# Second products ahead of the third pass, an earlier weight split and three relus on VectorE in a fused attention and mixture-of-experts kernel

## The chip, the cores and the metric

The kernel runs on one core of one Trainium2 chip. The core has TensorE (PE, matrix products into PSUM), VectorE (DVE), ScalarE (ACT), GpSimd (POOL) and SyncE (SP, which here only issues transfers). Each works through its own instructions in its own order, and semaphores tie them together. The metric is the device time of one execution in microseconds; the time of a kernel is the median over its runs.

## The reference

Polynomial attention without a softmax, and then a dense mixture of four experts on its output. Shapes: 4 batches, 4 heads, 1088 positions of 32 values, so 4352 tokens of 128 values; w1 is 4 x 128 x 1024 and w2 is 4 x 1024 x 128, all float32.

```python
phi(x) = outer(S1 @ x, S2 @ x).reshape(64)
kv = einsum('bhsf,bhsd->bhfd', phi(k), v);  z = sum(phi(k), axis=2)
x  = (phi(q) @ kv) / (phi(q) @ z + 1e-6)      # then heads side by side: (4352, 128)
p  = domain_probs / (domain_probs.sum(-1) + 1e-9)
out = sum over e of p[:, e] * (relu(x @ w1[e]) @ w2[e])
```

## The kernel before, in words

The 4352 tokens are worked in 11 chunks (128, 448, 512, seven times 448, 128). A chunk goes through 16 steps, four for each expert e; step i makes two 128-wide blocks of hidden values, j = 0 and j = 1. So (20,1) below is the second block of step 20, and steps 16 to 31 are chunk 1: 16 to 19 expert 0, 20 to 23 expert 1, 24 to 27 expert 2. `NQ` is 16, `NP` is 4.

**First product.** In chunks 1 to 9 the product x @ w1 is made of three fast passes on pieces of the operands (xa, xb, xd and wa, wb, wd). Function `first` issues the first two passes for (i,j) on TensorE (L1133, L1134), then ScalarE scales the PSUM tile in place (L1135). The third pass (L1182, in `third`) adds onto the scaled tile. It is issued one half step later, so that other matmuls lie between: within `first` for (i,j), `third()` issues the third pass of the half step before, and after it ScalarE takes the relu (L1190 into `hid`, or L1185 into `ha`; VectorE then makes the low parts `hb`, L1159, and `hd`, L1162, in `lower`).

**Second product.** The hidden blocks are multiplied by w2 later, from a list `due` sorted by half step. `to_due` enters them; `behind(at)` issues what is due by half step `at`. It is called through `between(0)` after the first half of a step and again after `first`. Chunk 0 is worked in plain float32 (L1111 relu, L245 products, L1218 on VectorE, L1223 the store of the result tile `end`); its last products are due in steps 16 and 17. In chunk 1 experts 0 and 1 have one float32 product per block (`whole`, L1231), due at half steps 2i + 3 + j. From expert 2 of chunk 1 on, each pair of blocks is dealt as short passes `a`, `b`, `d` and `x` by the table `DEAL` (L1250).

**Weights.** w2 is split into parts by `second_weight_parts(e)`, in two calls a few steps apart: the first makes the upper and lower parts (ScalarE L907, then two VectorE L910 `vab`, `vb`), the second the rest (L907, two L910 `vd`). `W2_AT` holds the steps of the two calls for the experts 2, 3, 0 and 1, and they are issued after `first` of that step:

```python
    W2_AT = (18, 19), (20, 21), (22, 23), (26, 32)
...
        for step in at:
            at_step(step, next_of(parts_of))
```

**Attention beside it.** The attention of later tokens is a list of pieces, `plan`, of which `work()` runs some in every half step. For one group of queries: a projection on TensorE (L245, `qT,sx`), a copy on ScalarE (L771, `qs`), a store to DRAM (`qd`, L773), loads in widened form (`qp`, L778, and `qb`, L783; ten issues on SyncE for the first group), two products on VectorE (L792, one for each half of the heads), the product with the key sums on TensorE (L245, `kvx,qp`), and division and transposes on VectorE. PSUM holds six banks for the tiles named `h` and one each for `o0` and `o1`. Order on each engine's queue is the order in which the program records the instructions; nothing is reordered later.

Of the kernel before, what the change touches and what calls it, by code (L numbers as in the profile page):

```python
# [12 lines left out]
ALU = mybir.AluOpType  # L13
ACTF = mybir.ActivationFunctionType
# [10 lines left out]
def kernel(  # L25
# [24 lines left out]
    nc = tc.nc  # L50
# [11 lines left out]
    NQ = E * FB // 2  # L62
# [20 lines left out]
        ("b", 1, 1, 16), ("d", 1, 1, 17), ("b", 2, 0, 16), ("d", 2, 0, 17), ("b", 2, 1, 17), ("d", 2, 1, 18),  # L83
        ("a", 3, 1, 17), ("b", 3, 0, 19), ("d", 3, 0, 19), ("b", 3, 1, 20), ("d", 3, 1, 20),
    ]
    W2_AT = (18, 19), (20, 21), (22, 23), (26, 32)
    TOKENS_AT = 11, 12

    CHUNKS = [P, 448, 512] + [448] * 7 + [P]
# [13 lines left out]
    def psum(pool, tag):  # L103
        return pool.tile([P, 512], F32, tag=tag, name=tag)
# [64 lines left out]
    def in_three(b):  # L169
        return b in THREE  # L170
# [76 lines left out]
    def both(out, weights, moving, **flags):  # L247

        for _ in range(2):
            on_side(lambda s: out[half[s], :], lambda s: weights[:, half[s]], lambda s: moving, **flags)  # L250
# [129 lines left out]
    def placed(c, n):  # L380

        for a, z, t, off in PLACES:
            lo, hi = max(c, a), min(c + n, z)
            if lo < hi:
                yield t[:, off + lo - a : off + hi - a], lo - c, hi - lo
# [526 lines left out]
    def weight_part(what, e, h):  # L912

        c = slice(F // 2 * h, F // 2 * (h + 1))
        w, a, b, d = (x[:, c] for x in (w1_of[e], wa[:, e], wb[:, e], wd[:, e]))
        if what == "a":
            split(a, w, 4096.0)
        elif what == "b":
            join(b, w, -4096.0, a.bitcast(F32), ALU.add)
        else:  # L920
            join(d, a.bitcast(F32), -R12, b.bitcast(F32), ALU.subtract)
# [134 lines left out]
    hid, acc, total = {}, {}, {}  # L1056
    NP = FB // 2

    def plain(m):
        return m in (0, NC - 1)  # L1060

    def whole(m, e):
        return m == 1 and e < E // 2

    def three_first(m, e):
        return not plain(m)
# [3 lines left out]
    def half_columns(i, hp, c):  # L1070

        e, f = divmod(i, NP)
        for j in range(2):
            both(
                hp[:, P * j + c : P * j + c + HP],
                w1_of[e][:, P * (2 * f + j) : P * (2 * f + j + 1)],
                x_first[:, c : c + HP],
                start=True,
                stop=True,
            )  # L1080

    def first(i, work, between=None):

        m, kq = steps[i]
        n, (e, f) = CHUNKS[m], divmod(kq, NP)
        if plain(m):
            third()
            lower()
            hd = hidden()
            hid[i] = [hd[:, n * j : n * j + n] for j in range(2)]  # L1090
            if i in begun_hp:
                hp = begun_hp.pop(i)
                half_columns(i, hp, HP)
            elif i in made_hp:
                hp = made_hp.pop(i)
            else:
                hp = psum(ps_h, "h")
                for j in range(2):
                    both(
                        hp[:, n * j : n * j + n],  # L1100
                        w1_of[e][:, P * (2 * f + j) : P * (2 * f + j + 1)],
                        (x_last if m else x_first)[:, :],
                        start=True,
                        stop=True,
                    )
            if m and kq % 2:
                nc.vector.tensor_scalar(
                    out=hd[:, 0 : 2 * n], in0=hp[:, 0 : 2 * n], scalar1=0.0, scalar2=None, op0=ALU.max
                )
            else:  # L1110
                nc.scalar.activation(hd[:, 0 : 2 * n], hp[:, 0 : 2 * n], ACTF.Relu)  # L1111
            work()
            work()
            return
        hid[i] = []
        if not three_first(m, e):
            ((x, _, _),) = placed(START[m], n)
            for j in range(2):
                hp = psum(ps_h, "h")[:, 0:n]
                nc.tensor.matmul(hp, w1_of[e][:, P * (2 * f + j) : P * (2 * f + j + 1)], x, start=True, stop=True)  # L1120
                u = hidden()[:, 0:n]
                nc.scalar.activation(u, hp, ACTF.Relu)
                hid[i].append(u)
                work()
                if j == 0:
                    between(0)
            return
        xa, xb, xd_ = (x[:, 0:n] for x in xparts[m])
        for j in range(2):
            k = 2 * f + j  # L1130
            g = psum(ps_h, "h")[:, 0:n]
            w = slice(P * k, P * (k + 1))
            nc.tensor.matmul(g, wa[:, e, w], xa, start=True, stop=False)  # L1133
            nc.tensor.matmul(g, wb[:, e, w], xb, start=False, stop=True)  # L1134
            nc.scalar.activation(g, g, ACTF.Copy, scale=1.0 + R12)  # L1135
            third()
            hid[i].append(None)
            begun.append((i, j, k, g, wd[:, e, w], xd_))

            if any(d[0] <= 2 * i + j and d[5] and d[5] + str(2 * (steps[d[3]][1] % NP) + d[4]) == last_of[1] for d in due):  # L1140
                between(j)
                lower()
                work()
            else:
                lower()
                work()
                if j == 0:
                    between(0)

    def hidden():  # L1150
        return mpool.tile([P, CW], F32, tag="hid", bufs=4, name="hid")
# [3 lines left out]
    def lower():  # L1155

        while to_lower:
            g, high, hb, both_of = to_lower.pop(0)
            nc.vector.scalar_tensor_tensor(out=hb, in0=g, scalar=0.0, in1=high, op0=ALU.max, op1=ALU.subtract)  # L1159
            if both_of:  # L1160
                a2, b2, d2 = both_of
                nc.vector.scalar_tensor_tensor(  # L1162
                    out=d2, in0=a2.bitcast(F32), scalar=R12, in1=b2.bitcast(F32), op0=ALU.mult, op1=ALU.subtract
                )
# [3 lines left out]
    def three_tiles(k, n):  # L1168

        t = split_at(k)  # L1170
        if t % 2 == 0:
            pair_of[0] = [
                mpool.tile([P, 2, CW], F32R, tag=f"h{i}", bufs=2, name=f"h{i}")[:, :, 0:n] for i in "abd"
            ]
        return tuple(x[:, t % 2] for x in pair_of[0]), pair_of[0] if t % 2 else None

    def third():

        while begun:
            i, j, k, g, w, x = begun.pop(0)  # L1180
            n = g.shape[-1]
            nc.tensor.matmul(g, w, x, start=False, stop=True, skip_group_check=True)  # L1182
            if in_three(k) and not whole(steps[i][0], steps[i][1] // NP):
                (ha, hb, hc), both_of = three_tiles(k, n)
                nc.scalar.activation(ha, g, ACTF.Relu, scale=NEAR)  # L1185
                to_lower.append((g, ha.bitcast(F32), hb, both_of))
                hid[i][j] = ha, hb, hc
            else:
                hid[i][j] = hidden()[:, 0:n]
                nc.scalar.activation(hid[i][j], g, ACTF.Relu)  # L1190

    def second(i, j=None):

# [152 lines left out]
    def at_step(step, *calls):  # L1346
        to_part.setdefault(step, []).extend(calls)
# [4 lines left out]
    for what, e, h, step in SPLITS:  # L1352
        at_step(step, lambda p=(what, e, h): weight_part(*p))
    for e, at in zip((2, 3, 0, 1), W2_AT):
        parts_of = second_weight_parts(e)
# [21 lines left out]
    due, closed = [], [None]  # L1377
# [16 lines left out]
    def to_due(i):  # L1394

        m, kq = steps[i]
        e, f = divmod(kq, NP)
        if plain(m):
            due.append((2 * i + 5, 2 * i, 0, i, None, None))
        elif whole(m, e):  # L1400
            due.extend((2 * i + 3 + j, 2 * i, j, i, j, None) for j in range(2))
        elif f == 0:
            for at, (p, slot) in enumerate(DEAL.items()):
                k = int(p[1])
                due.append((2 * i + slot, 2 * i, at, i + k // 2, k % 2, p[0]))
        due.sort(key=lambda d: d[:3])

    for i in range(len(steps) + LA):
        if i < len(steps):
# [11 lines left out]
            def work():  # L1421

                now[0] += 1
                if not NQ <= i < NQ + 2:
                    credit[0] = min(credit[0] + rate * rooms[min(now[0], len(rooms) - 1)], 0.5)
                if holds[0]:
                    credit[0] = max(credit[0], 0.01)
                while credit[0] > 0:
                    cost = piece()
                    credit[0] -= cost  # L1430
                    if not cost:
                        break

            first(i, work, lambda j: behind(2 * i + j))
            to_due(i)
            if kq == NQ - 4 and 0 < m < NC - 2:
                until_there(START[m + 1] + CHUNKS[m + 1])
# [57 lines left out]
```

## Time and profile before

| What | Value |
|---|---|
| Median of 3 runs | 451.99 us (451.21 to 453.21) |
| The profiled execution | 452.88 us, its span 450.0 us |
| Granted TensorE clock | 1.00 over the span |
| TensorE, VectorE, ScalarE, GpSimd busy | 99%, 80%, 74%, 27% |
| DMA, mean over the span | 85 GB/s |
| L1133, L1134, L1182, one pass of 448 columns | 468, 368, 371 ns busy, 0.20 us from start to start |
| L1231, one float32 product of 448 columns | two rows of 545 ns |
| L1135 and L1190 on ScalarE, 128x448 | 540 and 552 ns |
| L1159 on VectorE, 128x448 | 624 ns |
| L1279 on VectorE, copy of 128x448 out of PSUM | 610 ns |

The rows of a timeline read: start, busy time in us, engine, line, operation, written tile <- read tiles, shape, count; in brackets the idle time of the engine before it and who ended it. Rows of TensorE overlap, since matmuls are pipelined: the step from one start to the next tells more than the busy time. Where two steps in one row are merged (x2, x32), the time is that of all. SPq is SyncE's queue of transfers: its rows are the issues, not the transfers.

### The profile page before, as it was taken

The numbers are of one execution on the slowest core, as the hardware profiler recorded it, in microseconds if no ns is written. First come the engines' busy times: TensorE is split into PE (matmuls) and PEld (weight loads), VectorE is DVE, ScalarE is ACT, GpSimd is POOL, SyncE is SP. The second block draws the span as 40 slices with busy tenths as digits, with TensorE's granted clock in tenths as the row PEclk, the third lists the DMA queues.
The fourth block names the chain that finished last, engine by engine and source line by source line (L and its number), as shares of the span: only waits on it lengthen the run. The fifth ranks groups of instructions, "written<-read, shape, count | busy, mean of one in ns | idle before, by whom it ended". The sixth has DMA issues, their size and how long they took to land.

```text
span 450.0 us, 8678 instructions
## 1 busy us (share of the span) xinstructions
PE 444.5 (99%) x3021; PEld 369.3 (82%) x3021; DVE 358.6 (80%) x608; ACT 332.5 (74%) x702; POOL 121.5 (27%) x209
## 2 busy tenths in 40 slices
PE   8999999999999999999999999999999999999997
PEld 5887678777778888888888888888888888888886
DVE  5997689787988896888879869787779787787753
ACT  4477788677867886778688767787788788877741
POOL 7344133310323132212321312134123212321320
PEclk9999999999999999999999999999999999999999
DMA  7954741115223302252242142410320121018401
GB/s 197 296 145 142 189 118 58 30 30 129 93 58 88 120 23 79 51 129 70 66 124 27 22 113 78 119 49 21 95 52 28 33 45 41 22 34 217 158 2 28
DMA packets 53780, 38.45 MB, mean 85 GB/s; under 512 B 26921, under 2 KB 49897, under 8 KB 53737
## 3 DMA queue, kind: packets, MB, share of 16 engines
q1 hardware_dynamic: 53064, 37.77, 31.6%
q8 instruction: 23, 0.38, 0.4%
q0 software_dynamic: 448, 0.07, 0.2%
q14 instruction: 21, 0.16, 0.1%
q10 hardware_dynamic: 224, 0.07, 0.1%
HBM read 32.68 MB, written 5.21 MB: 84 GB/s over the span
## 4 chain that ended last, share of the span: by engine, by line
PE 94%; DVE 3%; DMA 1%; issue 1%; ACT 0%; SPq 0%; DVEq 0%
PE o L1250 39%; PE h L1182 13%; PE h L1133 13%; PE h L1134 13%; PE h L245 9%; PE o L245 3%; PE o L1231 3%; PE h L440 1%; DMA kn<-in_k_dram 1%; DVE hb L1159 1%; DVE qp L593 0%; DVE hd L1162 0%; DVE qa L882 0%; DVE rd L625 0%; DVE kp L456 0%
## 5 line engine op out<-in xcount | busy, mean ns | idle before, releaser
L1135 ACT ACTIVATE h<-h 128x448 f32<-128x448 f32 (+1 forms) x288 | 155.3, 540 | 79.0 <-PE h L1134 73.9
L1159 DVE SCALAR_TENSOR_TENSOR hb<-h,ha 128x448 fp32r<-128x448 f32 (+1 forms) x204 | 125.9, 624 | 55.8 <-ACT ha L1185 54.7
L1133 PE MATMUL h<-xa,wa 128*128 128x448 f32 (+1 forms) x288 | 134.9, 468 | 0.0
L1162 DVE SCALAR_TENSOR_TENSOR hd<-ha,hb 128x896 fp32r<-128x896 f32 (+1 forms) x102 | 116.0, 1137 | 8.2
L1185 ACT ACTIVATE ha<-h 128x448 fp32r<-128x448 f32 (+1 forms) x204 | 111.5, 547 | 0.0
L1182 PE MATMUL h<-xd,wd 128*128 128x448 f32 (+1 forms) x288 | 106.9, 371 | 0.2 <-ACT h L1135 0.2
L1134 PE MATMUL h<-xb,wb 128*128 128x448 f32 (+1 forms) x288 | 105.9, 368 | 0.0
L1289 POOL TENSOR_TENSOR ev<-ev,gate 128x256 f32<-128x256 f32 (+1 forms) x54 | 40.8, 756 | 219.8 <-DVE ev L1282 201.3
L1250 PE MATMUL o<-ha,vab 128*128 128x448 f32 (+1 forms) x204 | 76.4, 374 | 0.0
L1133 PEld LDWEIGHTS h<-xa,wa 128*128 128x128 f32 x288 | 54.2, 188 | 19.8 <-issue 14.6
L1134 PEld LDWEIGHTS h<-xb,wb 128*128 128x128 f32 x288 | 54.2, 188 | 19.5 <-issue 15.5
L1250 PE MATMUL o<-hid,w_sb 128*128 128x448 f32 (+1 forms) x136 | 63.0, 545 | 0.0
L1182 PEld LDWEIGHTS h<-xd,wd 128*128 128x128 f32 x288 | 54.0, 187 | 9.9 <-ACT h L1135 3.0
L1250 PE MATMUL o<-hd,vd 128*128 128x448 f32 (+1 forms) x204 | 58.8, 369 | 0.0
L1250 PE MATMUL o<-hb,vb 128*128 128x448 f32 (+1 forms) x136 | 49.9, 368 | 0.3 <-DVE hb L1159 0.3
L1291 POOL TENSOR_TENSOR total<-total,ev 128x256 f32<-128x256 f32 (+1 forms) x54 | 46.6, 864 | 4.2
L1190 ACT ACTIVATE hid<-h 128x448 f32<-128x448 f32 (+1 forms) x84 | 46.4, 552 | 0.2
L1250 PEld LDWEIGHTS o<-ha,vab 128*128 128x128 f32 x204 | 38.3, 188 | 4.2 <-issue 0.2
L1250 PEld LDWEIGHTS o<-hd,vd 128*128 128x128 f32 x204 | 38.1, 188 | 3.4
L1289 POOL TENSOR_TENSOR total<-ev,gate 128x256 f32<-128x256 f32 (+1 forms) x18 | 12.2, 699 | 75.6 <-issue 56.4
L1250 PEld LDWEIGHTS o<-hb,vb 128*128 128x128 f32 x136 | 25.5, 188 | 2.7 <-DVE hb L1159 0.7
L1250 PEld LDWEIGHTS o<-hid,w_sb 128*128 128x128 f32 x136 | 25.5, 188 | 2.5 <-DVE ev L1282 0.3
(141 smaller groups left out, 436.7 us busy)
## 6 DMA issues: line engine op xcount, KB each, us to landing
gate<-gates SPq DMA_DIRECT2D x24, 224.0 KB
kn<-in_k_dram SPq DMA_DIRECT2D x4, 544.0 KB
vn<-in_v_dram SPq DMA_DIRECT2D x16, 128.0 KB
w_last<-in_moe_w_dram SPq DMA_DIRECT2D x4, 512.0 KB
w_sb<-in_moe_w_dram SPq DMA_DIRECT2D x3, 512.0 KB
w_sb<-in_moe_w_dram SPq DMA_DIRECT2D x6, 256.0 KB
qp<-qd SPq DMA_DIRECT2D x6, 224.0 KB
qb<-qd SPq DMA_DIRECT2D x6, 224.0 KB
```

The costliest lines, as they stand in the source:

```text
L245: nc.tensor.matmul(out(s), weights(s), moving(s), **flags)
L1133: nc.tensor.matmul(g, wa[:, e, w], xa, start=True, stop=False)
L1134: nc.tensor.matmul(g, wb[:, e, w], xb, start=False, stop=True)
L1135: nc.scalar.activation(g, g, ACTF.Copy, scale=1.0 + R12)
L1159: nc.vector.scalar_tensor_tensor(out=hb, in0=g, scalar=0.0, in1=high, op0=ALU.max, op1=ALU.subtract)
L1162: nc.vector.scalar_tensor_tensor(out=d2, in0=a2.bitcast(F32), scalar=R12, in1=b2.bitcast(F32), op0=ALU.mult, op1=ALU.subtract)
L1182: nc.tensor.matmul(g, w, x, start=False, stop=True, skip_group_check=True)
L1185: nc.scalar.activation(ha, g, ACTF.Relu, scale=NEAR)
L1190: nc.scalar.activation(hid[i][j], g, ACTF.Relu)
L1250: nc.tensor.matmul(acc[m, e][o][:, 0:n], w, h, start=first_one, stop=last)
L1289: nc.gpsimd.tensor_tensor(out=to[:, x], in0=ev[:, x], in1=g[:, x], op=ALU.mult)
L1291: nc.gpsimd.tensor_tensor(out=total[m][:, x], in0=total[m][:, x], in1=ev[:, x], op=ALU.add)
```

## The change

1. In steps 16 and 17 `first` calls `between(j)` ahead of `third()`, so second products that are due come ahead of the third pass.
2. The first call of `second_weight_parts` for expert 1 moves from step 26 to step 24; the second stays in step 32.
3. In steps 20, 21 and 22 the relu of block j = 1 is a VectorE instruction.
4. The product of the last block of expert 1 (step 23, j = 1) is due one half step later, at 51 instead of 50.

```diff
-    W2_AT = (18, 19), (20, 21), (22, 23), (26, 32)
+    W2_AT = (18, 19), (20, 21), (22, 23), (24, 32)
...
             nc.scalar.activation(g, g, ACTF.Copy, scale=1.0 + R12)
+            if i < NQ + 2:
+                between(j)
             third()
...
                 hid[i][j] = hidden()[:, 0:n]
-                nc.scalar.activation(hid[i][j], g, ACTF.Relu)
+                if NQ + NP <= i < NQ + 2 * NP - 1 and j:
+                    nc.vector.tensor_scalar(
+                        out=hid[i][j], in0=g, scalar1=0.0, scalar2=None, op0=ALU.max
+                    )
+                else:
+                    nc.scalar.activation(hid[i][j], g, ACTF.Relu)
...
         elif whole(m, e):
-            due.extend((2 * i + 3 + j, 2 * i, j, i, j, None) for j in range(2))
+            late = e and f == NP - 1
+            due.extend((2 * i + 3 + j + (j if late else 0), 2 * i, j, i, j, None) for j in range(2))
```

The lines after these edits have higher numbers in the changed kernel; the text before the result uses those of the kernel before. The number of instructions and transfers of the whole program is the same; three change their engine.

## Prediction

> **What bounds the kernel now.** First the page's parts 1 and 2.
>
> ```profile
> PE 444.5 (99%) x3021; PEld 369.3 (82%) x3021; DVE 358.6 (80%) x608; ACT 332.5 (74%) x702; POOL 121.5 (27%) x209
> PEclk9999999999999999999999999999999999999999
> ```
>
> TensorE is busy 99% at full clock, so only its gaps can be won. Next, TensorE's timeline from 28 to 76 us. A 128x448 pass starts 0.20 us after the one before; larger steps between two starts are gaps.
>
> ```profile
> 29.38 0.37 PE L1134 MATMUL h<-xb,wb 128*128 128x448 f32 x1
> 29.95 0.47 PE L1182 MATMUL h<-xd,wd 128*128 128x448 f32 x1 [0.21 <-ACT h L1135]
> ...
> 31.86 0.36 PE L1134 MATMUL h<-xb,wb 128*128 128x448 f32 x1
> 32.23 0.47 PE L1182 MATMUL h<-xd,wd 128*128 128x448 f32 x1
> ...
> 60.59 0.36 PE L1134 MATMUL h<-xb,wb 128*128 128x448 f32 x1
> 60.96 0.47 PE L1182 MATMUL h<-xd,wd 128*128 128x448 f32 x1
> ...
> 67.11 0.36 PE L1182 MATMUL h<-xd,wd 128*128 128x448 f32 x1
> 67.79 0.47 PE L1250 MATMUL o<-hb,vb 128*128 128x448 f32 x1 [0.32 <-DVE hb L1159]
> ```
>
> The four gaps are 0.37, 0.17, 0.17 and 0.48 us over the pitch, and each costs about 0.11 more, since the instruction after a stall also starts late: 0.48, 0.28, 0.28, 0.59. All the change can win here is 1.63 us, 0.36% of the run. The profiled run took 452.88 us (span 450.0), 0.89 above the median of 451.99; I work differences out in its trace and add them to the median. A measurement of this kernel can tell about 0.5% (2.26 us) from no change.
>
> Third, what else holds this stretch: VectorE, TensorE and SyncE's queue around 52 us.
>
> ```profile
> 48.31 0.61 DVE L1279 COPY ev<-o 128x448 f32<-128x448 f32 x1
> 52.11 0.69 DVE L792 TENSOR_TENSOR qp<-qp,qb 128x512 f32<-128x512 f32 x1 [3.19 <-DMA qb<-qd]
> 52.72 0.42 DVE L910 SCALAR_TENSOR_TENSOR vd<-vab 128x256 fp32r<-128x256 f32 x1
> 53.06 0.68 DVE L910 SCALAR_TENSOR_TENSOR vd<-vb,vab 128x512 fp32r<-128x512 f32 x1
> 53.66 0.42 DVE L910 SCALAR_TENSOR_TENSOR vab<-w_sb,vab 128x256 fp32r<-128x256 f32 x1
> ```
> ```profile
> 52.33 1.22 PE L245 MATMUL h<-kvx,qp 128*64 128x66 f32 x32
> 53.48 1.02 PE L1231 MATMUL o<-hid,w_sb 128*128 128x448 f32 x2
> ```
> ```profile
> 34.89 1.16 SPq L773 DMA_DIRECT2D qd<-qs  x2
> 40.85 0.59 SPq L778 DMA_DIRECT2D qp<-qd  x1
> ...
> 47.50 0.63 SPq L1223 DMA_DIRECT2D out_dram<-end  x1
> 48.23 0.53 SPq L118 DMA_DIRECT2D kn<-in_k_dram  x1
> ```
>
> VectorE stands 3.19 us at the second L792 until a transfer lands at 52.1. TensorE's L245 on qp starts at 52.33; its second half needs that product, done at 52.80. The group takes 1.15 us to the next start, 1.03 at 101.03. So TensorE reaches this product just when the transfer lets it: a hidden wall.
>
> **The change part by part**
>
> *Products ahead of the third pass, steps 16 and 17.* The order of the changed program puts four L245 (0.58 us) between L1134 at 29.38 and L1182, and in step 17 four L245 and an L1231 between 31.86 and L1182. Their inputs are early (the L1111 relus end by 28.72, the L1190 by 31.0). They fill the time in which ScalarE's L1135 runs. Gain 0.48 + 0.28 = 0.76. Moved with them: L771's projection starts some 0.3 us later, L1218 runs earlier on VectorE, and SyncE's 64 KB store of `end` (L1223) goes from after the qb loads to before the qd stores.
>
> *The gain meets the wall.* The landing hangs on SyncE's chain (gates at 30.48, qn at 34.42, qd, a wait until 40.85, ten issues to 47.39), which follows VectorE's transpose at 30.15 and not TensorE. So the wall does not come earlier, and 0.76 turns into waiting: net 0.
>
> *The store moves the wall later, by s.* In SyncE's queue it takes 0.73 us (47.50 to 48.23), so the qd stores are issued that much later: upper end 0.73. The stores landed 4.80 us after their last issue (36.05 to 40.85), the next pair 1.96 (55.69 to 57.65), so some 2.8 us are backlog; if it hides the late issue, only the bytes count: 64 KB at the 243 GB/s of 36 to 40 us, 0.27. Nothing starts earlier, so no gain. I take the middle, 0.5. [...]
>
> *Three relus on VectorE: (20,1), (21,1), (22,1).* The changed order puts the first ahead of the first L792, the second behind the second L792 and both vd, the third two L910 later. A relu of 128x448 out of PSUM is bounded by hb (0.54 to the next start) and the copy of 48.31 (0.61); I take 0.61, the same access. First: free slot at 47.6 (46.8 with the gain), needed by L1231 at 48.71 (47.95): hidden, margin 0.5. Third: ends near 55.8 + s, needed at 56.30 plus the delay below: hidden. Second: L792 at 52.11 + s, then the rows' own pitch to 53.66 + s, then 0.61: done at 54.27 + s. Its product is the L1231 of 53.48. With 0.04 for the signal it starts at 54.31 + s: **+0.83 + s = +1.33**. That VectorE does not overtake is seen in the first vd: its ScalarE split ended at 49.06, and it waited to 52.72. [...] ScalarE loses three times 0.45 us, none of it on the path: the small gap at 47.03 hangs on L907, which waits for VectorE's wb.
>
> *Split of the second expert in step 24, and its last product half a step later.* ScalarE:
>
> ```profile
> 58.16 0.54 ACT L1185 ACTIVATE ha<-h 128x448 fp32r<-128x448 f32 x1
> 59.02 0.53 ACT L1135 ACTIVATE h<-h 128x448 f32<-128x448 f32 x1 [0.32 <-PE h L1134]
> ```
>
> The L907 (0.74 to the next start) now comes between these: 58.62 to 59.36. So L1135 starts at 59.36, not 59.02, and its L1182 at 59.90. TensorE, with the L1231 moved from ahead of it, would be there at 59.43: a gap of 0.47 + 0.11 = 0.58. The moved L1231 then fills the old gap at 60.96 (0.28). Net **+0.30**. On VectorE the two L910 of this split go ahead of the hb of 60.03: 0.87 us more until 65.78. The nearest user, the bank freed by L1279 at 61.70, was due on TensorE at 62.90; copy and user both arrive near 63.2, so cover is about nil, and every 0.1 the copy is late costs 0.1. At 65.78 two L910 (1.34 us to 67.12) drop out, so the hb of 67.12 comes 0.47 earlier while TensorE comes 0.30 later: 0.77 against a gap of 0.48. It goes: **−0.59**.
>
> Sum: 1.33 + 0.30 − 0.59 = **+1.04**. The trace would give 453.92; the median 451.99 + 1.04 = **453.0 us**.
>
> **Rivals**
>
> *The transfer lands early, the wall is not met (faster).* If L792 starts by 50.5 us (52.73 for L1231 less 0.04, 0.61 and 1.55), the relu is in time and all gains stay: −0.76 + 0.30 − 0.59 = −1.05: 450.9. Below that point each 0.1 us earlier than 52.1 is worth 0.1. For it: this trace is 0.89 over the median, and a transfer's landing can differ between executions. Against: ten issues of 0.6 us by one queue set most of it, and the store comes ahead. 0.20.
>
> *The loads collide (clearly slower).* With the store gone from between, the 544 KB load kn follows the last qb issue at once instead of 0.84 us later, while qb took 4.7 us from that issue to landing. A collision costs up to its 2.3 us at 243 GB/s. Every 0.1 us later is 0.1 us on TensorE; from s = 1.7 the run is slower by over 2.26. With s of 1.2 to 2.8: 453.7 to 455.3. For it: 350 to 408 GB/s are already moving at 50.4 to 51.1. Against: the qb loads stand ahead in the same queue. 0.20.
>
> *The VectorE work moved to step 24 spoils its own gain.* If the copy and hb are 0.6 us later than worked out, the −0.59 turns to about 0: 453.6. It lies in the range, with the forecast's chance.
>
> **How the numbers follow.** Forecast 0.60: s from 0 to 1.1 and the step-24 term 0 to 0.6 worse give 452.5 to 454.2. The early landing reaches to 450.9, the collision to 455.3. Leaving out the lower tenth and the upper tenth: 451.0 to 454.7. Slower by over 2.26 (454.25): 0.12 of the collision, 0.05 of the forecast, 0.17. Faster by over 2.26 needs more than all the gaps; 0.03 for the runs' spread of 2.0 us. Same: 0.80.
>
> **What would show it.** Right: no gaps after L1134 near 29.4 and 31.5; TensorE waiting at L245 on qp and then at L1231 near 54 us for a VectorE relu, the largest single wait after 20 us; L1223 ahead of L773 in SyncE's queue and the second L792 past 52.1; a gap of about 0.5 near 60 (plus the delay) and none at hb near 68. Wrong: the second L792 at 50.5 or earlier, or a relu that starts before it. The direction fails then; the size fails if L792 starts more than 1 us from 52.6.

## The result, and the profile after

The changed kernel takes 453.86 us, the kernel before 452.05 (medians of 19 runs each): a ratio of 1.0036, 95% interval 1.0019 to 1.0053, so 1.8 us slower. The forecast was 453.0 in a range of 451.0 to 454.7. The profiled execution took 455.28 us, its span 452.5. The lines of the changed kernel are numbered two to seven higher: L1182 is now L1184, L1231 is L1238, L1250 is L1257, L1223 is L1230, and the new relu on VectorE is L1193.

From the page:

```profile
PE 444.7 (98%) x3021; PEld 369.8 (82%) x3021; DVE 359.7 (79%) x611; ACT 331.2 (73%) x699; POOL 121.8 (27%) x209
...
PEclk9999999999999999999999999999999999999999
```

The granted clock reads 9 (90% or more) in each of the 40 slices, as before; slices of 11 us hide what the windows below show. TensorE's timeline (start, busy, engine, line, operation, tiles; in brackets the idle time and who ended it):

```profile
28.99 0.37 PE L1134 MATMUL h<-xb,wb 128*128 128x448 f32 x1
29.28 0.66 PE L245 MATMUL o<-w_sb,hid 128*64 128x128 f32 x8
...
50.72 0.98 PE L245 MATMUL h<-qT,sx 128*64 128x224 f32 x8
...
53.45 0.69 PE L245 MATMUL h<-kvx,qp 128*64 128x66 f32 x16 [1.29 <-DVE qp L792]
54.93 1.86 PE L1238 MATMUL o<-hid,w_sb 128*128 128x448 f32 x2 [0.78 <-DVE hid L1193]
...
62.87 0.47 PE L1184 MATMUL h<-xd,wd 128*128 128x448 f32 x1 [0.27 <-ACT h L1135]
...
70.40 0.36 PE L1184 MATMUL h<-xd,wd 128*128 128x448 f32 x1
70.60 0.37 PE L1257 MATMUL o<-hb,vb 128*128 128x448 f32 x1
```

The waits of 1.29 and 0.78 us, at 53.45 and 54.93, were not there before. The second products stand behind L1134, and the gaps near 30 and 32 us are gone, but less was won than the length of these gaps. The same projection stood before at

```profile
51.52 0.98 PE L245 MATMUL h<-qT,sx 128*64 128x224 f32 x8
```

From the first L1133 of the stretch (28.66 before, 28.27 after) to this row TensorE took 22.86 us before and 22.45 after: 0.41 less, where the two gaps had been put at 0.76. It is the second gap that brought nothing: from its L1134 (31.86 before, 30.99 after) to the next L1134 behind the L1231 (35.14 and 34.34) the same rows took 3.28 us before and 3.35 after. There the third pass now stands between two groups of float32 products which stood together before; that this is the cause was not tried. What was won is waited away at 53.45, and the relu costs another wait at 54.93. The gap of step 24 is there (62.87), and the one at hb is not (0.20 from 70.40 to 70.60). The L1238 at 54.93 is busy for 1.86 us where the same product took 1.02: that is not a wait. VectorE, and two issues on SyncE's queue:

```profile
52.71 0.69 DVE L792 TENSOR_TENSOR qp<-qp,qb 128x512 f32<-128x512 f32 x1 [3.11 <-DMA qb<-qd]
53.32 0.42 DVE L910 SCALAR_TENSOR_TENSOR vd<-vab 128x256 fp32r<-128x256 f32 x1
53.65 0.68 DVE L910 SCALAR_TENSOR_TENSOR vd<-vb,vab 128x512 fp32r<-128x512 f32 x1
54.26 0.61 DVE L1193 TENSOR_SCALAR hid<-h 128x448 f32<-128x448 f32 x1
```
```profile
34.49 0.66 SPq L1230 DMA_DIRECT2D out_dram<-end  x1
...
47.55 0.39 SPq L118 DMA_DIRECT2D kn<-in_k_dram  x1
```

The relu starts right behind the second L792 and both `vd`, as worked out, and TensorE 0.06 us after its end. The store of `end` is now ahead of the qd stores, and kn follows the last qb issue at once. What made L1238 long is in the windows of 1 us (window, length; PE busy (instructions), PEld, DVE, ACT, POOL; the granted clock; DMA share, GB/s):

```profile
54.00:55.00 1.00, 0.22 (x7) 0.08 (x2) 1.00 (x3) 0.00 (x0) 0.00 (x0) 0.90 0.84 172
55.00:56.00 1.00, 1.00 (x3) 0.59 (x3) 1.00 (x3) 0.00 (x0) 0.00 (x0) 0.50 0.58 133
...
58.00:59.00 1.00, 1.00 (x4) 0.50 (x4) 0.00 (x0) 1.00 (x3) 0.00 (x0) 0.89 0.00 0
```

The clock is the column before the DMA share. It reads 0.50 in the two windows left out as well, so it stays there for 0.20 + 3 + 0.22 = 3.42 us, which is 1.7 us of TensorE's work. The rows from the L1238 at 54.93 to the L1133 at 61.08 took 6.15 us, the same rows before 4.59 (53.48 to 58.07): 1.56 longer. Nothing like it was forecast. The mean clock of each run shows how often it came: 12 of the 19 runs have 0.999 or 1.000, median 453.1, and 7 have 0.994 to 0.996, median 455.3. A mean of 0.997 to 0.999 is not counted as such a fall: the one kept trace with 0.997 ("the group's product later" below) has the clock at 1.00 in every window of 10 us up to 450 of its 454.2 us, and no run of the kernel before beside the experiments (101 runs on four chips) lies below 0.997. The first group is 1.05 above the kernel before, which is the size of the forecast (1.04).

In the trace of after, waits of 1.29 and 0.78 us, 0.70 us apart, stand right ahead of the 3.42 us at 0.50. By the mean clock such a fall came in 7 of the 19 runs only; what decides when, no run here shows.

### The profile page after: what moved, and what is told of

The parts are those of the page before. It is cut to its first block, busy times and chain, and to the rows that moved or that the text cites. A ratio compares the mean times of both kernels' runs of the same rounds, so it can differ in the third digit from the quotient of the medians.

```text
span 452.5 us, 8680 instructions
## 1 busy us (share of the span) xinstructions
PE 444.7 (98%) x3021; PEld 369.8 (82%) x3021; DVE 359.7 (79%) x611; ACT 331.2 (73%) x699; POOL 121.8 (27%) x209
## 4 chain that ended last, share of the span: by engine, by line
PE 94%; DMA 2%; DVE 1%; ACT 1%; issue 0%; SPq 0%; POOL 0%; DVEq 0%; ACTq 0%
PE o L1257 40%; PE h L1184 13%; PE h L1133 13%; PE h L1134 13%; PE h L245 9%; PE o L245 3%; PE o L1238 2%; PE h L440 1%; DMA qb<-qd 1%; SPq L783 0%; DMA s_raw<-in_S_dram 0%; ACT h L1135 0%; DVE qp L593 0%; DVE vd L910 0%; DVE kp L462 0%
## 5 line engine op out<-in xcount | busy, mean ns | idle before, releaser
L1135 ACT ACTIVATE h<-h 128x448 f32<-128x448 f32 (+1 forms) x288 | 155.4, 540 | 82.3 <-PE h L1134 72.2
L1133 PE MATMUL h<-xa,wa 128*128 128x448 f32 (+1 forms) x288 | 135.1, 469 | 0.0
L1184 PE MATMUL h<-xd,wd 128*128 128x448 f32 (+1 forms) x288 | 107.3, 373 | 0.3 <-ACT h L1135 0.3
L1134 PE MATMUL h<-xb,wb 128*128 128x448 f32 (+1 forms) x288 | 106.1, 369 | 0.0
L1257 PE MATMUL o<-ha,vab 128*128 128x448 f32 (+1 forms) x204 | 76.4, 374 | 0.0
L1133 PEld LDWEIGHTS h<-xa,wa 128*128 128x128 f32 x288 | 54.4, 189 | 20.2 <-issue 15.2
L1134 PEld LDWEIGHTS h<-xb,wb 128*128 128x128 f32 x288 | 54.4, 189 | 19.5 <-issue 15.6
L1257 PE MATMUL o<-hid,w_sb 128*128 128x448 f32 (+1 forms) x136 | 62.9, 544 | 0.0
L1184 PEld LDWEIGHTS h<-xd,wd 128*128 128x128 f32 x288 | 54.1, 188 | 9.6 <-ACT h L1135 2.3
L1257 PE MATMUL o<-hd,vd 128*128 128x448 f32 (+1 forms) x204 | 58.8, 369 | 0.0
L1257 PE MATMUL o<-hb,vb 128*128 128x448 f32 (+1 forms) x136 | 49.9, 368 | 0.0
L1197 ACT ACTIVATE hid<-h 128x448 f32<-128x448 f32 (+1 forms) x81 | 44.8, 553 | 0.9 <-PE h L1184 0.8
L1257 PEld LDWEIGHTS o<-ha,vab 128*128 128x128 f32 x204 | 38.3, 188 | 4.2 <-issue 0.2
L1257 PEld LDWEIGHTS o<-hd,vd 128*128 128x128 f32 x204 | 38.1, 188 | 3.5
L1257 PEld LDWEIGHTS o<-hid,w_sb 128*128 128x128 f32 x136 | 25.5, 188 | 2.3
L1257 PEld LDWEIGHTS o<-hb,vb 128*128 128x128 f32 x136 | 25.6, 188 | 2.0
```

Source lines behind the costliest of these rows:

```text
L1257: nc.tensor.matmul(acc[m, e][o][:, 0:n], w, h, start=first_one, stop=last)
```

## The experiments

Ratios are against the kernel before, run on the same chip in the same session.

**The first part alone.** The kernel before with one edit:

```diff
+            if i < NQ + 2:
+                between(j)
             third()
```

> The kernel before with edit 1 alone (products due ahead of the third pass in steps 16 and 17). Theory (a wall at the second L792, set by transfers, and moved later by the store that comes ahead): the 0.76 us gained at 29 to 32 us is gone again at the L245 on qp, which waits 1.2 to 1.4 us there; the wall itself is 0.6 to 1.0 us later, so the run is 0.5 to 1.0 us slower than before: 452.5 to 453.0 beside 452.0. No wait at L1231 and the TensorE clock stays at 1.00. Rival (the relus and the step-24 edits are the whole cost, and the first edit pays): no such wait, 0.76 us faster, 451.3.

Measured: 452.59 (12 runs), ratio 1.0009 (0.9996 to 1.0022), clock 0.999 or above in all. TensorE's waits, then VectorE:

```profile
PE h L245 <- DVE qp L792: 1.2, 1, 1.2
```
```profile
52.78 0.69 DVE L792 TENSOR_TENSOR qp<-qp,qb 128x512 f32<-128x512 f32 x1 [3.20 <-DMA qb<-qd]
```

Two gaps of TensorE are filled and one wait of 1.2 us stands at the landing. TensorE reached the second projection at 22.45 us of the stretch, as in the whole change, 0.41 earlier than before. The interval reaches just below no change, but not to this gain, which would be a ratio of 0.9991.

**The relus alone.** The kernel before with the three relus on VectorE.

```diff
-                nc.scalar.activation(hid[i][j], g, ACTF.Relu)
+                if NQ + NP <= i < NQ + 2 * NP - 1 and j:
+                    nc.vector.tensor_scalar(out=hid[i][j], in0=g, scalar1=0.0, scalar2=None, op0=ALU.max)
+                else:
+                    nc.scalar.activation(hid[i][j], g, ACTF.Relu)
```

> The kernel before with edit 3 alone (three relus on VectorE). Theory: the store stays behind the qb loads and the second L792 starts near 52.1 as before; the relu of (21,1) stands behind it and two L910, and L1231 waits for it: +0.83 us, 452.9 beside 452.0, with one TensorE wait of 0.7 to 0.9 us for VectorE. Rival (the store moved ahead and the lost clock are the whole cost, the relus are hidden): no wait at L1231, 452.0, or slightly faster for the relief of ScalarE.

Measured: 452.48 (12 runs), ratio 1.0014 (1.0000 to 1.0028). TensorE's timeline:

```profile
54.38 1.02 PE L1236 MATMUL o<-hid,w_sb 128*128 128x448 f32 x2 [0.78 <-DVE hid L1191]
```

The wait is there at the forecast size without the other parts. The time went up by 0.54, and the forecast 0.83 lies inside the interval.

**Step 24 alone.** The kernel before with the earlier split and the last product of expert 1 half a step later.

```diff
-    W2_AT = (18, 19), (20, 21), (22, 23), (26, 32)
+    W2_AT = (18, 19), (20, 21), (22, 23), (24, 32)
...
+            late = e and f == NP - 1
+            due.extend((2 * i + 3 + j + (j if late else 0), 2 * i, j, i, j, None) for j in range(2))
```

> The kernel before with edits 2 and 4 alone (first call for expert 1 in step 24, its last product at half step 51). Theory: the gap at 60.96 (0.28) becomes one of about 0.58 near 59.9, the one at 67.79 (0.59) goes: -0.29 us, 451.75 beside 452.0. Rival (the VectorE work moved ahead delays the copy L1279 and the hb, and spoils its own gain): a wait for VectorE near 63 and 452.0 to 452.4.

Measured: 451.84 (12 runs), ratio 1.0000 (0.9986 to 1.0014). ScalarE, then TensorE:

```profile
68.59 0.63 ACT L907 ACTIVATE xa<-ring 128x512 fp32r<-128x512 f32 x1 [0.53 <-DMA ring<-xd]
```
```profile
69.71 0.47 PE L1182 MATMUL h<-xd,wd 128*128 128x448 f32 x1 [0.43 <-ACT h L1135]
```

The gap at hb goes, and a gap of the same size comes 2 us later: ScalarE's next piece of work waits for the transfer that brings the next chunk's tokens (`ring`), and the L1135 behind it is late. The kernel before had that wait as well (0.36 at 68.65), hidden by the gap at hb. In the whole change the same L907 at 71.46 waits for nothing, because TensorE is some 3 us later by then. So in these traces the −0.59 holds beside the delay and not by itself. The times can't tell: the interval holds the expected −0.29 us as well as nothing.

**The relu behind the landing back on ScalarE.** The whole change with only (20,1) and (22,1) on VectorE.

```diff
-                if NQ + NP <= i < NQ + 2 * NP - 1 and j:
+                if i in (NQ + NP, NQ + NP + 2) and j:
```

> The changed kernel with the relu of (21,1) back on ScalarE; those of (20,1) and (22,1) stay on VectorE. Theory: the wait of the L245 on qp stays (1.2 to 1.4 us), the wait at L1231 is gone, and the clock stays at 1.00 because TensorE stands still once and not twice: moved wall 0.6 to 1.0, +0.30 and -0.59 from step 24: 0.3 to 0.7 us slower than before, 452.4 to 452.7, and 1.1 to 1.5 below the changed kernel's 453.9. Rival (the order on VectorE does not matter, the transfer alone does): 453.5 to 453.9 as the changed kernel.

Measured: 452.77 (12 runs), ratio 1.0026 (1.0007 to 1.0045). The wait at L1238 is gone, and one wait for VectorE is left:

```profile
PE h L245 <- DVE qp L792: 1.6, 1, 1.6
```

Eight of the 12 runs have the full clock, median 452.44, as expected. Two have 0.994 and 0.996 (455.7 and 455.2). I had expected no such run: a single wait of about 1.6 us seems to cost the clock at times, while the 1.2 us of the first part alone did not in 12 runs. The trace that was kept has the full clock, so where it fell in those two is not shown. The other two have 0.997 (453.4 and 454.3), which is not counted as a fall here.

**The store behind the loads.** The whole change with the store of `end` issued in step 17, after the qp and qb loads.

```diff
-                    nc.sync.dma_start(bass.AP(out.tensor, out.offset + t * DM, to), total.pop(m)[:, :])
+                    store = lambda z=total.pop(m): nc.sync.dma_start(bass.AP(out.tensor, out.offset + t * DM, to), z[:, :])
+                    if m:
+                        store()
+                    else:
+                        at_step(NQ + 1, store)
```

> The changed kernel, but the store of end is issued behind the ten qp and qb loads, as in the kernel before; the products stay ahead of the third pass. Theory (the store moves the wall): the second L792 starts 0.6 to 1.0 us earlier than in the changed kernel for the same start of the stretch, the L245 on qp waits 0.3 to 0.7 us and not 1.3, L1231 still waits 0.8 for the relu, TensorE stands still less, the clock falls in fewer runs: 452.6, some 1.2 below the changed kernel. Rival (the loads that follow decide the landing, not the store): the wait stays at 1.2 or more, 453.9.

Measured: 452.41 (12 runs), ratio 1.0006 (0.9994 to 1.0018); one run with the clock at 0.996. VectorE:

```profile
51.08 0.69 DVE L792 TENSOR_TENSOR qp<-qp,qb 128x512 f32<-128x512 f32 x1 [2.54 <-DMA qb<-qd]
```

The landing is 1.6 us earlier than in the whole change, TensorE does not wait at L245 any more, and of the two waits only the relu's is left (0.69). An exact size of the store's part in the landing can't be given: in the executions with the store behind (the kernel before, the relus alone, step 24 alone and this one) the second L792 started at 52.11, 52.16, 50.96 and 51.08, with it ahead at 52.71 (whole change), 52.78 (first part alone), 52.80 (without the middle relu) and 53.48 (the next experiment). The means, 51.58 and 52.94, are 1.4 us apart, over the forecast's upper end of 0.73 for s, and the same order spreads by about 1 us.

What the store does on SyncE's queue can be told, from the first qp load (before: 40.85, in the prediction). In the whole change:

```profile
40.99 0.58 SPq L778 DMA_DIRECT2D qp<-qd  x1
```

Counted from the first L1133 of the stretch, this issue comes at 12.10 to 12.19 us in the four executions with the store behind, and at 12.72 to 12.79 in the four with it ahead: 0.60 later. The rest comes after the last qb issue: from its end to the second L792 went 4.1 to 4.9 us with the store behind and 5.1 to 5.7 with it ahead.

**The waits filled.** The whole change with small bf16 products into a PSUM bank that is idle then, six ahead of the second half of the group's product and four after it. They add nothing to the output.

```diff
+                for _ in range(6 if fill is not None and p else 0):
+                    nc.tensor.matmul(fill[:, :], warm[:, 0:P], warm[:, :], start=True, stop=True)
```

> The changed kernel with useless bf16 matmuls (constant operands, an idle PSUM bank) where TensorE stands still: six ahead of the second half of the L245 on qp, four ahead of L1231. It measures what the fall of the clock costs. Theory (the clock falls because TensorE stands still twice within a few us): the work still waits as long for VectorE, but the granted clock stays at 0.999 or 1.000 in every run and the median is that of the changed kernel's runs with that clock, 453.1. Rival (the clock falls for another reason, by chance): 0.994 to 0.997 in a third of the runs as before and a median of 453.9 or more.

Measured: 452.89, ratio 1.0018 (1.0008 to 1.0028), all 12 runs between 452.54 and 453.38 at a clock of 0.999 or 1.000. The waits are still spent, on work of no use, and the time is that of the runs of the whole change with the full clock (453.1). So the fall of the clock hangs on TensorE's standing still (none of 12 runs with the waits filled, 7 of 19 with the waits), and most of what the median of the whole change lies above the forecast is the clock. The whole change itself was not run on that chip; the two kernels of the next experiment were, and lost the clock there.

**The group's product later.** Two tries to move the product off the landing: the whole change, and the first part alone, with the group's product on TensorE two half steps later (in the whole change the second L792 as well) and the next chunk's token pieces two steps later, since they follow it. The lines are those of the first; the second has 5 in place of 4 and leaves the product on VectorE where it was.

```diff
-                add(vector_us(n), lambda w=w, p=p: unit_product(w, p), "product", ("visit", LAND if w else LAND + 1))
+                add(vector_us(n), lambda w=w, p=p: unit_product(w, p), "product", ("visit", LAND if w else LAND + 1 + 2 * p))
...
-            add(0.1, visit, "visit", ("products" if last else "product", 3))
+            add(0.1, visit, "visit", ("products" if last else "product", 3 if w else 4))
...
-        for step in (NQ * m - 4, NQ * m - 3):
+        for step in (NQ * m - 4 + (2 if m == 2 else 0), NQ * m - 3 + (2 if m == 2 else 0)):
```

> The changed kernel with the second L792 two half steps later in VectorE's order (behind the relu of (21,1)), the L245 on qp with what hangs on it two half steps later on TensorE, and the operand parts of chunk 2 made in steps 30 and 31 instead of 28 and 29. Theory: TensorE meets neither the wall nor the relu; the gains stay: -0.76 + 0.30 - 0.59 = -1.05 us against before, 450.9, and the clock stays at 1.00. Rival (the gain is given back by the chain behind it, y, the store xd, the load of ring, L907 on ring): a wait on ScalarE for ring or on TensorE near 75 to 80 us and 451.9 or more.

> The kernel before with edit 1 alone, and the L245 on qp with what hangs on it two half steps later, chunk 2's operand parts in steps 30 and 31. Theory: with the wall out of TensorE's way the first edit pays in full: -0.76 us, 451.2 beside 452.0, and the gap at hb near 68 stays or shifts. Rival (the first edit's gain is lost at another wait): 451.9 to 452.4.

Measured (6 runs each): 456.15, ratio 1.0088 (1.0069 to 1.0107), and 457.76, ratio 1.0113 (1.0093 to 1.0133). Both expectations were wrong by over 5 us; the rival of the first, a wait near 75 to 80 us from the chain behind the product, is nearest to what came. TensorE's timeline of the first:

```profile
80.89 0.47 PE L1184 MATMUL h<-xd,wd 128*128 128x512 f32 x1 [2.04 <-DVE xd L910]
```

The wait at L245 is gone in both, but the pieces xb and xd of the next chunk, which the shift delayed, come 0.5 to 0.9 and 2.0 us late at the start of that chunk. The clock falls again, but not each time: 8 of the 12 runs have a mean of 0.991 to 0.996. The kept trace of the second, with waits of 0.86 and 2.04, has a mean clock of 0.83 from 80 to 90 us, and its passes of 448 columns start 0.37 us apart (81.93 to 82.30, 84.33 to 84.70) and not 0.20; that of the first, with waits of 0.52 and 2.04, has the clock at 1.00 there. Nothing is learned about the landing from these two, except that the tokens have no room for two steps.

**Two queues.** If the landing of the second half is the wall, bringing it forward must give the gain back. The four qb loads of that half are issued on GpSimd's queue, which stood idle from 39.3 to 49.0 us, in three kernels: the first part alone, the whole change, and the kernel before.

```diff
-                nc.sync.dma_start(
+                (nc.gpsimd if p and w == 0 else nc.sync).dma_start(
                     qb[p][32 * x : 32 * x + 32, 0:n],
```

> The kernel before with the second products ahead of the third pass alone (as in first_alone, 452.6), and the four qb loads of the first later unit's second half issued on GpSimd's queue in place of SyncE's, where four issues took 2.53 us. Theory (the landing of the second half is the wall that takes the gain): SyncE issues that half's qp right behind the first half's qb, the last load is issued by 45.2 in place of 47.7, and lands some 2.5 us earlier; the second L792 starts before 50.5, TensorE doesn't wait for it at L245, the two gains of 0.48 and 0.28 stay, and the time is 0.5 to 0.8 below the kernel before, about 451.2. Rival (the landing is set by the loads that are under way beside it, the key and value loads that now start 2.5 us earlier among them): the second L792 stays beyond 52, the wait of 1.2 us stays, about 452.5. Second rival: the visit's TensorE work is limited by something else of the visit, and another wait of 0.5 to 1.2 us takes its place: about 452.

> The whole change, with the same four qb loads on GpSimd's queue. Theory: with the second L792 before 50.5, TensorE's waits of 1.29 at L245 and 0.78 at L1238 both go, because the relu of (21, 1) on VectorE no longer stands behind a waiting instruction, and with them the granted clock of 0.50, so that no run lies above 454; left are -0.76 of the products ahead and the gap of step 24 of 0.3 to 0.5: about 451.4, which is 2.4 below the whole change as it was. Rival (the clock falls for another reason than the two waits): times above 454 in a third of the runs. Rival (the relus cost by VectorE's load, not by the landing): the wait at L1238 stays at 0.6 to 0.8 and the time is about 452.3.

> The kernel before with nothing but the four qb loads on GpSimd's queue. Theory: the kernel before has no wait of TensorE on L792, so an earlier landing is worth nothing by itself: within 0.3 of the kernel before. Rival (the landing costs in the kernel before as well, by what is queued behind the second L792 on VectorE): 0.5 or more faster, and then two_queues_first owes that much to the loads and not to the products.

Measured, in one session (kernel before: 451.71; 12 runs of each of the three): 451.31, ratio 0.9985 (0.9971 to 1.0000); 451.07, ratio 0.9982 (0.9969 to 0.9996); 451.98, ratio 1.0005 (0.9993 to 1.0017). No run of the three has a clock below 0.998. The whole change, VectorE and TensorE:

```profile
49.42 0.69 DVE L792 TENSOR_TENSOR qp<-qp,qb 128x512 f32<-128x512 f32 x1
...
51.91 0.61 DVE L1193 TENSOR_SCALAR hid<-h 128x448 f32<-128x448 f32 x1
```
```profile
52.78 1.02 PE L1238 MATMUL o<-hid,w_sb 128*128 128x448 f32 x2
```

The second L792 starts at 49.42 and waits for nothing, the relu ends at 52.52, and TensorE waits neither at L245 nor at L1238. The changed kernel, with only four loads issued on another queue (kn and the value loads then go out 2.6 us earlier as well), went from 1.8 us slower to 0.6 us faster than the kernel before of its own session. TensorE in the kernel before with the loads moved:

```profile
47.64 0.47 PE L1182 MATMUL h<-xd,wd 128*128 128x448 f32 x1 [0.76 <-ACT h L1135]
```

So that kernel is no clean zero: it has a wait of 0.76 us that the kernel before does not have. The first part alone has it too (0.90), which is more than the 0.41 that it wins up to there: its trace reaches the L245 on qp at 24.15 us of the stretch, the kernel before at 23.67. What edit 1 is worth with the early landing is therefore read between these two kernels, which differ by it alone: 0.67 us by the medians, 0.72 by the means (0.27 to 1.17, by drawing anew from the 12 runs of each).

**Two queues, the loads behind the copies.** On GpSimd the loads stood ahead of two copies of the values (L406), which so ran at 44 to 46 us beside VectorE's splits. Here the copies come first again, as in the kernel before; the lines that follow have numbers eight higher (L910 is L918).

```diff
+                if p and w == 0:
+                    pool_loads.append(load)
+                else:
+                    load(nc.sync)
...
         copy(vx[0:64, 8, :, 0:D], _ap(vn[b], 0, 64, 1024, [[D, H], [1, D]]))
+        while pool_loads:
+            pool_loads.pop(0)(nc.gpsimd)
```

> As two_queues_all, but on GpSimd the two copies of the values (L406, L411 there) stand ahead of the four loads, as in the kernel before, and no longer run beside VectorE's wb and wd. In two_queues_all they ran from 43.9 to 46.3 beside wb and wd, which took 0.90 and 0.98 (0.65 and 0.69 in the kernel before), and TensorE waited 0.25 at the third pass at 46.46. Theory (VectorE's instructions stretch while GpSimd works on tiles in SBUF): the copies run at about 37.4 to 39.3, wb takes 0.65 and wd 0.69 again, the wait at 46.5 goes, the second L792 stays before 50.5; some 0.3 below two_queues_all, about 450.8 where the kernel before has 451.7. Rival (VectorE's wb and wd were slow for another reason, the loads of qb on GpSimd's queue among them): they stay at 0.9 or more, and the time stays at 451.1.

Measured: 450.89 (9 runs; kernel before in that session 452.42), ratio 0.9977 (0.9958 to 0.9996), about 1.0 us below the kernel before by the ratio. VectorE's wb in the first part with two queues:

```profile
44.56 1.55 DVE L910 SCALAR_TENSOR_TENSOR wb<-w_sb,wa 128x512 fp32r<-128x512 f32 x1
```

Here the instruction, at 44.22, is back at 0.65 us, and the wait of TensorE at 46.5 to 47.6 that followed (0.25 in the whole change, 0.90 in the first part; 0.76 in the kernel before, where two `vd` took 0.77 and 1.10) is gone. TensorE reaches the L245 on qp at 23.26 us of the stretch without waiting, and the product of the relu at 24.33; the kernel before is there at 23.67 and 24.82. The difference in time to the whole change with two queues, 0.0005 of the ratio, is too small to be told.

## Why the prediction was right, and where its sizes were off

- *Products ahead, and the wall.* Right that the landing takes the gain back (first part alone) and that SyncE's chain does not follow TensorE: it starts 1.82 us into the stretch before and after (30.48 and 30.09). With the early landing edit 1 pays (first part against kernel before, both with two queues). The gain itself was put too high: 0.76 in the prediction, 0.41 in the traces, since the second gap brought nothing. The sum does not show it, because there the gain becomes waiting; the early-landing rival's 450.9 rests on it.
- *The store moves the wall by s.* The right sign, too small. The trace of after starts this stretch 0.39 us earlier (L1133 at 28.27, before at 28.66), so the second L792 at 52.71 is 0.99 later by its own start, where s was taken as 0.5, with 0.73 as the upper end. The late issue itself was sized well: 0.60 us on SyncE's queue, between the bounds of 0.27 and 0.73. What the bound missed: it counted only the issue that is put ahead, but from the last qb issue to the second L792 went 5.3 us (47.45 to 52.71), before 4.7. The load kn, which now follows at once, may be the cause; no run takes that load away.
- *The second relu.* Right in place and size. L1238 was forecast at 53.48 + 0.83 + s; with s = 0.99 and the earlier start that is 54.91, and it started at 54.93.
- *Step 24.* The gap: 0.58 forecast, 0.53 measured (0.43 over the pitch and 0.10 behind it). The gain at hb: right in the whole change, but its reason was incomplete. ScalarE's wait for `ring`, which already stood in the trace of before at 68.65, was not looked at; in the part alone the gap comes back 2 us later.
- *The term that was missing: the granted clock.* The forecast counted two waits at their length. In about a third of the runs (7 of 19) the clock fell as well, which cost 1.56 us in the trace. From the start of the stretch to the pass of hb the trace of after is 70.60 − 67.79 + 0.39 = 3.20 us longer. The forecast to that point is 1.33 + 0.30 − 0.48 = 1.15; with 0.49 more for s and 1.56 for the clock it is 3.20.
- *What was luck.* The runs with the full clock lie 1.05 above the kernel before, where the sum says 1.04. In the trace the terms without the clock come to 3.20 − 1.56 = 1.64 and not to 1.15, and one landing differs from the next by about 1 us, so an agreement to 0.01 is partly chance.
- *The rivals.* The early landing decides the sign, as its point of 50.5 us said, and the loads on two queues made it happen: the second L792 at 49.4, and 0.8 to 1.0 us faster by the ratios, where 1.05 was forecast. The collision was priced from s = 1.2 on: the means with the store ahead and behind are 1.4 apart, so its lower edge was met, where the forecast had given it 0.20; what collides was not tried. The loss of 0.36% lies under the bound of 0.5%, as forecast, though with 19 runs of each its interval leaves out no change.

## What to carry to other kernels

Before work is moved into a gap, look for the next thing on the path that does not move with it: here a transfer that was just hidden, and a gain of 0.4 us became a wait. A filled gap is worth its length only if the rows around it keep their pace: of two gaps one brought nothing. An instruction moved to another engine is priced by what stands ahead of it in that engine's queue, and if that is a wait for a transfer, by the landing: here the relu on VectorE started at 54.26, behind an L792 that stood until 52.71. Bring the landing forward before making more work hang on it: with four loads on another queue that L792 started at 49.42. Short waits of TensorE close together can cost more than their length: here 1.29 and 0.78 us were followed by 3.42 us at a clock of 0.50, which cost 1.56 us more.

## What the runs showed of the hardware that was not expected

- In the trace the clock was halved for 3.42 us after waits of 1.29 and 0.78 us. By the mean clock (0.996 or less) it fell in 7 of 19 runs with these waits, in 2 of 12 with one of about 1.6 us, in 1 of 12 with one of 0.69 us (the store behind the loads), in none of 12 with one of 1.2 us, and in none of 12 when products of no use filled the waits; where it fell in the runs without a trace is not shown. Nearly the same waits need not cost it: after 0.52 and 2.04 us one trace kept a clock of 1.00, after 0.86 and 2.04 another had a mean of 0.83 from 80 to 90 us.
- Some rows of VectorE's L910 took longer beside GpSimd's copies and sums of tiles: wb 1.55 us in place of 0.65 (the first part with two queues, beside the copies at 44.4 to 46.3), and vd of 128x256 0.96 in place of 0.42 (the whole change with two queues, beside the sum at 49.5 to 51.4). Not all did: in the kernel before, xd of 128x512 at 73.44 took 0.69 beside a GpSimd product from 73.60 on, and xb of 128x512 at 70.58, with no work of GpSimd beside it, 0.68. What makes the difference, no row here shows.
- The same chain of small transfers landed between 50.96 and 52.16 us in four executions of four kernels with the same order on SyncE's queue, 22.7 to 23.6 us into the stretch: what hangs on a landing has a spread of about 1 us.
